# Attention and a gated MLP on one core: the same steps in another order on every engine

## The chip, the cores and the metric

The kernel runs on one core of one Trainium2 chip. The time is device microseconds of one execution, from its start to its end on the core; the median of several executions is compared. The inputs lie in HBM, and so does the output at the end. TensorE (PE) multiplies, VectorE (DVE), ScalarE (ACT) and GpSimd (POOL) work on tiles in SBUF, and SyncE (SP) issues all the transfers (DMAs) of this kernel. Each engine works through its own instructions in order.

## What is computed

For 4 batches, 8 heads and 768 positions of width 64, each chunk of 32 positions attends to 8 memory keys, the 16 positions before it, its own 32 and the 8 behind it. The result, 4 x 768 x 512, goes through a gated MLP with a mixing over positions:

```
scores = 0.125 * q_c @ concat(mem_k, k_ctx).T        # per chunk of 32 queries
a      = softmax(scores);  x = a @ concat(mem_v, v_ctx)
h      = gelu_tanh(x @ w_in)                          # 512 -> 1024
u, v   = h[..., :512], h[..., 512:]
v_n    = (v - mean(v)) / sqrt(var(v) + 1e-6) * g_ln
v_s    = w_sg @ v_n + b_sg                            # over the 768 positions
out    = x + (u * v_s) @ w_out
```

## The kernel before

The large products run in fp32r as three products of parts: each operand is split into a rounded part (hi) and its residue (lo), and hi*lo, lo*hi and hi*hi are accumulated in one PSUM bank (`product`, with `HL`). The residue costs a copy (hi, on ACT) and a subtraction (lo, on DVE or POOL).

All work is cut into 1186 named steps. `step(name, does, *eng)` puts each into a table with its engine, and a few steps with a second engine. The string `ORDER` at the top of the file lists the names; the loop at the end of `conformer_kernel` takes them one after the other and emits their instructions. `InOrder` pins that order, so the order in `ORDER` is the order in which every engine, SP's queue of DMA issues among them, meets its instructions. A star behind a name picks the step's second engine. No planner runs at build time; semaphores are put in from the data that the steps read and write.

The names that matter here:

- `ri<h><k>` loads a 512 KB piece of `w_in` (half h, rows k) as integers. `d3`, `d2`, `d5`, `d6` (ACT, then three DVE passes) turn a piece into fp32, `d8` rounds it (ACT), `d9` makes the residue. For the four pieces `i10` to `i13`, which the V products need, the residue is made on TensorE: `Xi10` and so on subtract by two products, and `d9` only copies from PSUM on ACT. `ro` and `d.o` do the same for `w_out`; `g`, `ga`, `gb` load and split a block of `w_sg`.
- Attention goes by units u = 0 to 23 (6 per batch, 128 positions and 8 heads each). `q<u>`, `k<u>`, `v<u>` load. `S<u>` are the scores: 64 small matmuls, each with its own weight load. `mx`, `sb` (DVE) take the maximum and subtract it, `ex` is Exp on ACT, `z` clears outside keys, `sm`, `sr` (DVE) give the sum and its reciprocal, `nm` multiplies (DVE, or POOL with a star). `T<u>` transposes on TensorE, `p<u>` copies the result to SBUF, `A<u>` multiplies by the values (64 small matmuls with loads). `xc`, `xh`, `xl` copy and split x. `S` of the next unit waits for `sb` of this one, since both touch the same PSUM tile.
- Batch b: `V<b><tt>` is x times the second half of `w_in` for 128 positions, `v1` its Gelu, `v5`, `vx`, `vy`, `v6`, `v7` the normalisation (`v6` on POOL), `v8`, `v9` the split. `U<b><h><j>` is the first half for 384 positions, `u1` its Gelu. `W<b><h><j>` (batches 0 and 1) is the product with `w_sg`, `w1` and `w2` scale and gate it, `w3`, `w4` split it, `O<b><h><j>` is the product with `w_out`, `o1` adds it to x, `out` stores it.
- Batches 2 and 3 take a recombined form of the `w_sg` product: `M<b><term><j>` for seven terms, `mr`, `mt`, `md` (DVE, POOL) add them up, `c1` to `c4`, `sh`, `sl` make the left operands. `y..` steps make the recombined `w_sg` blocks and keep them in HBM.
- `zz<n>` are products of the identity whose result nobody reads.

PSUM has four banks for the products T, X, V, U, W, M and O. `mms` is a queue of free banks: a product takes the first of it, and the step that reads the result last gives the bank back. All steps are emitted in the order of the list, so a product must wait until the step that gave its bank back has run.

```
for i, name in enumerate(names):
    ...
    does, eng = steps.pop(name.rstrip("*"))
    does(eng[name.endswith("*")])
```

Of the kernel before, what the change touches and what calls it, by code (L numbers as in the profile page):

```python
# [51 lines left out]
w2013 w3013 d8o0 d6o2 sm10 d8o2 T8 d9o0* xc7 w4003 w4002 ex11 w2000 w3000 p8 yl010 W012 W010 xc6 yc10 w1012 sb12 d9o2*
sr10 w4000 d9o3 A9 A8 w1010 w2012 w2010 w3010 ex12 yl110 yl100 yc30* z12 O002 O000 o1000 z11 sm11 w4010* nm10 O003
o1003 O001 v12 sm13 sm12 w4013 T10 w3012 w4011 w4012 O013 sr11 xc8 xh6 xc9 xh7 xl7 o1013 yc20 yh50 ym50 k15 v11 out000
S15 k14 S14 O012 mx14 sr13 o1002 mx15 sr12 o1012 O010 xh8 xl8 nm11* o1001 xl6* sb14 T11 o1010 V10 nm13* v110 v510 vx10
sb15 k16 ys50 q17 k17 O011 ex14 p10 q16 V12 ex15 xh9 V11 A10 v112 yh70 yh60 yc40* nm12* yh40 ym60* p11 A11 v111 xl9
ym40 yl001 ys60 T12 p12 o1011 v512 vx12 vy12 v511 xc10 xh10 xc11 V13 vy10 xh11 xl11 v610 v612 v712 v812 xl10 v710 v810
v912* ym70* v910 v113 v513 vx11 yl011 ys40 vx13 vy13 vy11 v613 v713 S16 S17 v813 U102 V15 U101 v115 u1102 v913* v515
V14 out001 U100 v14 yc11* yl111 ys70 q18 yc31* out002 k18 v13 u1101 v114 v611 v711 vx15 vy15 v615 v514 vx14 yh71 vy14
v715 v815 v811 yh51 v614 yc21* v911 T13 v714 v814 u1100 U103 U112 u1103 U111 sm14 mx16 ym51* sr14 p13* nm14* mx17 sb16  # L60
out012 ex16 A12 A13 v915 sm15 v914* W102 sm16 sb17 w1102 sr15 w2102 W100 w1100 w2100 out010 out003 k19 q19 yh61 xc12
w3102 yl101 yc41* ym71 W103 T14 S19 S18 yl002 ys51 k20 cg yl012 w1103 w2103 w4102 mx18 mx19 sb18 v15 W101 ym61* w1101
p14 ex17 w3100 w4100 z17 nm15* w3103 yc12* W112 ex18 u1112 yh41 u1111 w2101 T15 W110 sb19 w1110 ym41* w1112 ys71 yl112
U113 p15 yh52 W113 w3101 w4101 z18 sm18 u1113 xc13 W111 w2112 w1113 w2113 sr18 nm18 w4103* w1111 sm17 sr16 sr17 out013
yl102 yc32* yc22* ym52 A14 A15 O100 U110 q20 ys52 q21 w2111 u1110 w3113 w3111 k21 out011 v17 w2110 w3110 w4110* ys41
ex19 w3112 xc14 yh62 S21 S20 O102 ys61 q22 o1102 O103 nm17* db w4111* w4113 T17 w4112 o1100 p17* mx21 o1103 nm16 O101
o1101 sb21 yh72 O112 xh12 ex21 sm21 xc15 xl12 o1112 sm19 sr19 xh14 O111 T16 O113 yr52 q23 p16* sr21 xl14* v16 v18
out100 yc42* yh42 ym42 k22 yr50 A17 A16 nm19 ym72* o1113 mx20 o1111 T19 sb20 O110 T18 p18* v20 V20 xh13 xl13 V21 S22
xc16 ys72 k23 S23 xh15 ex20 p19 ym62 ys62 ys42 v120 xc17 xl15 mx22 yr51 sb22 sm20 xh17 v121 xh16 out102 v520 ex22 sm22
vx20 vy20 xl16 v620 nm21* V23 sr20 v123 V22 A18 v19 A19 v22 out101 v21 o1110 mx23 sb23 V24 v720 xl17 v521 vx21 out103  # L70
v122 nm20* T21 vy21 U201 ex23 v522 z23 v721 sm23 p21* vx22 vy22 v523 T20 u1201 v124 v622 vx23 v722 v524 vx24 sr23 v724
p20 v723 out113 out110 v621 out112 out111 V25 U200 vz21 xc19 vz20 vz22 vy23 nm23* vy24 sr22 v125 v525 vx25 v725 vy25
sh21 u1200 xc18 v624 v625 vz24 vz25 v623 vz23 nm22* c12* T23 U213 A20 u1213 A21 U203 T22 xc20 sl21* sh22 xc21 U211 p22
A22 c32 p23* v23 A23 yr71 yr60 yr62 yr61 sl22 M220 yr70 sh25 u1203 u1211 yr72 yr41 yr42 yr40 M210 c22* sh26 U202 u1202
sl25 sl26* c42 mr210 mr220 M221 sh24 M251 M211 sh27 mr211 sl27* mr221 M260 w2200* w3200 sl24* mr260 md20 M261 mr261
md21* mr251 sh23 M270 U212 u1212 mr270 M240 mr240 sl23* M271 w4200 M241 w2202 mr271 mr241 w2203 M250 U210 mr250 mt20
w3202 w3203 xc23 w2201 w4202* w3201 w4203* w4201 M230 M231 mt21 mr231 w2212 O201 w3212 mr230 w2211 w2213 o1201 w4212*
u1210 w2210 w3210 w3213 O200 w4213* w4210* w3211 w4211* O203 O202 xh18 xh19 xc22 o1203 O210 o1210 o1202 xl18* O213
O212 o1212 o1200 xl19 O211 xh20 xl20* V32 v132 v532 xh21 xl21* o1213 vx32 v732 V31 xh22 xh23 xl23 V30 v131 v130 v531
vx31 v731 V35 xl22* vy31 vy32 v632 vz32 v135 v535 vx35 vy35 v530 vx30 v730 vy30 V34 v134 v630 v631 v534 vx34 V33 v133  # L80
vz31 vz30 sh31 v635 v533 vx33 vy34 v634 out201 U312 o1211 vy33 v633 v734 v733 vz33 vz34 v735 vz35 c13 c33 u1312 U303
U301 U300 u1301 U302 u1303 sh32 out213 sl31* M310 out210 out212 u1300 sh35 M311 U313 c23 sh36 u1302 u1313 sl32* M321
sl35 M320 c43 sl36* mr310 mr320 sh37 sl37* w2300* w3300 sh34 mr311 mr321 sl34* M350 M361 mr361 md31* w2301* w3301 M371
M360 mr360 md30 mr371 mr350 sh33 M370 mr370 M340 mr340 mt30 M341 mr341 sl33 M351 M331 M330 w4301 w2303 w3303 w4303
mr351 mt31 w2313* w2312* mr330 out211 w2302 w3302 w4302* U310 u1310 w4300* w2310 mr331 U311 O303 O302 O301 u1311 w2311
w3312 w3310 w4310* O300 out200 w3313 w3311 o1303 o1301 w4311* o1300 out203 out300 w4312 w4313 O312 out303 out202
# [660 lines left out]
```

## Time and profile before

| what | value |
|---|---|
| median of 3 runs | 383.28 us (382.34 to 384.22) |
| the profiled execution | 382.99 us, span 381.2 us |
| TensorE busy | 364.7 us, 96% |
| DVE, ACT, POOL busy | 231.3, 168.0, 125.1 us |
| mean granted TensorE clock | 0.991 |
| DMA | 56.01 MB, mean 147 GB/s |
| TensorE's first instruction, its last product's end | 1.35 us, 377.4 us |
| wait of the first scores for their keys | 1.5 us |
| the four transposes of one T step | 0.58 us |
| packets of the queue `q8 instruction` | 37, 0.61 MB |

The span goes from the first to the last instruction of the program; the rest of the execution's time lies around it. Since nearly all steps are emitted from one line of a helper, the profile's line number is the same for all (L99), and groups are told apart by their tiles: `ma` to `mh` are the `w_in` pieces being decoded (`mc` is i12, `md` i13, `ma` i10, `mb` i11, `me` i00), `s` the scores, `av` the values' PSUM tile, `mma` to `mmd` the four PSUM banks. PEld are weight loads, PE the matmuls. The releaser that a wait names is inferred from semaphores, and is the last one to come by the profile, not always the true one. "issue" is waiting that no instruction of another engine explains. [...]

### The profile page before, as it was taken

The page shows a single profiled execution, that of the slowest core. Times are in us where ns is not written, and L with a number is a line of the kernel's source. Part 1 is how long each engine was busy: PE and PEld are TensorE (multiplying, and loading weights), DVE is VectorE, ACT ScalarE, POOL GpSimd, SP SyncE. Part 2 cuts the span into 40 slices and gives each one's busy share as a digit, 9 for nine tenths or more (in the row PEclk, how much of TensorE's full clock was granted, in tenths as well). Part 3 has the DMA queues.
Part 4 walks back from the last instruction along what each step waited for, and adds up shares of the span by engine and source line. Part 5 has one row for each costly group of instructions (what it writes and reads, how often), then busy time and mean ns, then how long its engine had stood idle before and what let it go on. Part 6 is the DMA issues. An engine that isn't in the chain of part 4 may idle for free.

```text
span 381.2 us, 10928 instructions
## 1 busy us (share of the span) xinstructions
PE 364.7 (96%) x4786; PEld 335.9 (88%) x4786; DVE 231.3 (61%) x420; ACT 168.0 (44%) x288; POOL 125.1 (33%) x138
## 2 busy tenths in 40 slices
...
GB/s 283 368 360 163 362 178 93 296 250 131 137 90 160 199 71 132 301 98 23 206 183 217 227 256 85 226 66 124 252 2 21 0 64 0 64 0 1 2 47 139
DMA packets 26063, 56.01 MB, mean 147 GB/s; under 512 B 3232, under 2 KB 13472, under 8 KB 26016
## 3 DMA queue, kind: packets, MB, share of 16 engines
q1 hardware_dynamic: 26016, 55.33, 42.5%
q8 instruction: 37, 0.61, 0.7%
...
## 4 chain that ended last, share of the span: by engine, by line
PE 88%; DVE 5%; ACT 2%; issue 2%; DMA 1%; SPq 0%; POOL 0%; ACTq 0%
PE mmc L99 23%; PE mma L99 19%; PE mmb L99 19%; PE mmd L99 16%; PE av L99 6%; PE s L99 4%; DVE vn L99 2%; DMA ka<-in_ks 1%; ACT L99 1%; ACT vn L99 0%; DVE me L99 0%; DVE eb L99 0%; DVE ea L99 0%; DVE mxa L99 0%; DVE paira L99 0%
## 5 line engine op out<-in xcount | busy, mean ns | idle before, releaser
L99 ACT ACT_TABLE_LOAD x20 | 25.7, 1283 | 9.1 <-DVE xa L99 4.8
L99 ACT CAST vh<-vn 128x768 fp32r<-128x768 f32 (+1 forms) x26 | 18.7, 736 | 18.6 <-DVE vn L99 10.3
L99 PE MATMUL mmc<-w_sg_hi,vh 128*128 128x384 f32 x120 | 25.5, 339 | 1.1 <-ACT uh L99 1.1
L99 DVE BATCH_NORM_STATS2 stats<-vn 128x6 f32<-128x512 f32 x24 | 16.4, 685 | 13.8 <-ACT vn L99 13.8
L99 POOL TENSOR_TENSOR stats<-stats,mhalf 128x1 f32<-128x1 f32 x24 | 15.2, 643 | 25.1 <-DVE stats L99 25.1
L99 PEld LDWEIGHTS mmc<-w_sg_hi,vh 128*128 128x128 f32 x120 | 21.0, 188 | 1.7 <-ACT uh L99 1.5
L99 DVE TENSOR_TENSOR vh<-vn,vh 128x768 fp32r<-128x768 f32 (+1 forms) x18 | 16.6, 927 | 5.7 <-ACT vh L99 5.7
L99 PEld LDWEIGHTS s<-ka,qa 64*32 64x32 f32 x768 | 8.6, 105 | 10.1 <-issue 5.0
L99 POOL TENSOR_TENSOR vh<-vn,vh 128x512 fp32r<-128x512 f32 (+1 forms) x8 | 13.3, 1663 | 10.1 <-ACT vh L99 10.1
L99 DVE TENSOR_SCALAR vn<-vn,stats 128x512 f32<-128x512 f32 x12 | 10.2, 854 | 9.5 <-POOL stats L99 9.5
L99 PE MATMUL s<-ka,qa 64*32 64x64 f32 x768 | 10.6, 225 | 5.3 <-DVE eb L99 2.1
L99 PE MATMUL mmb<-w_sg_hi,vh 128*128 128x384 f32 x66 | 14.1, 340 | 0.0
L99 PE MATMUL mmb<-w_in_hi,paira 128*128 128x512 f32 x48 | 13.2, 397 | 0.0
L99 PE MATMUL mma<-w_sg_hi,vh 128*128 128x384 f32 x60 | 12.9, 338 | 0.0
L99 PE MATMUL mmc<-w_sg_lo,vh 128*128 128x384 f32 x60 | 12.5, 334 | 0.0
L99 POOL TENSOR_TENSOR pairb<-xd,pairb 128x512 fp32r<-128x512 f32 x4 | 5.1, 1284 | 21.2 <-ACT pairb L99 21.2
L99 DVE TENSOR_TENSOR vn<-vn 128x768 f32<-128x768 f32 x6 | 8.9, 1480 | 5.3 <-POOL vn L99 3.8
L99 PEld LDWEIGHTS mmb<-w_sg_hi,vh 128*128 128x128 f32 x66 | 11.5, 188 | 0.2
L99 DVE SCALAR_TENSOR_TENSOR vn<-vn,stats,g_row 128x512 f32<-128x512 f32 x12 | 11.2, 954 | 0.1
L99 POOL TENSOR_TENSOR pairb<-xb,pairb 128x512 fp32r<-128x512 f32 x4 | 5.3, 1335 | 18.1 <-ACT pairb L99 18.1
L99 PE MATMUL mma<-pairb,w_out_hi 128*128 128x384 f32 x56 | 10.9, 335 | 0.0
L99 PEld LDWEIGHTS s<-kb,qb 64*32 64x32 f32 x768 | 8.4, 105 | 2.7 <-DVE ea L99 1.3
...
## 6 DMA issues: line engine op xcount, KB each, us to landing
...
```

What stands on the lines that cost most here:

```text
L99: return self.tc.keep_in_program_order(getattr(self.engine, name)(*args, **kw))
```

## The change

The list `ORDER` is replaced as a whole; nothing else is touched. Both lists hold the same 1186 names with the same three `zz` steps. They differ in the order on every engine, and in which steps carry a star. The start of the diff:

```diff
--- before.py
+++ after.py
 ORDER = """
-ri13 d3i13 d2i13 d5i13 q0 k0 d6i13 d8i13 zz8 S0 mx0 sb0 ex0 z0 sm0 sr0 nm0* k1 q1 ri11 zz4 ri12 S1 zz8 q2 k2 d3i11 mx1
-d2i11 d3i12 d2i12 d5i11 sb1 d5i12 ex1 d6i11 S2 T0 ri10 d3i10 p0 sm1 sr1 d6i12 v0 mx2 sb2 Xi13 A0 d2i10 d5i10 nm1* q3
-k3 d8i12 T1 S3 ex2 d9i13 d8i11 p1 xc0 xh0 mx3 sm2 sb3 d6i10 sr2 Xi12 q4 k4 Xi11 ex3 d9i11 d8i10 d9i12 S4 sm3 sr3 v1 A1
-Xi10 ri00 mx4 sb4 nm2* nm3* q5 k5 ri03 T2 T3 xh1 xl1 xl0 S5 d3i00 d2i00 d5i00 d9i10 p2 d3i03 p3 xc1 ex4 d6i00 mx5
-d2i03 d5i03 V01 v2 ri02 ri01 d6i03 sb5 d3i02 A2 xh2 ex5 d2i02 xl2 d5i02 V00 d8i00 d8i03 d3i01 z5 d9i00* d9i03* d2i01
-d5i01 d6i01 k6 q6 k7 q7 V02 S6 S7 v100 d8i01 d6i02 d8i02 v3 A3 v101 v102 g41 g00 d9i01* d9i02* g21 v5 g10 g01 g20 ga00
-xc3 xh3 ga21 v4 sm4 sr4 U000 U002 ga41 sm5 xl3 sr5 v500 vx00 nm4 mx7 v501 vx01 vy01 sb7 vy00 T4 U003 ro0 k9 q9 g50 g51
-k8 p4 ga20 gb00 nm5* T5 mx6 v600 gb20 ga10 xc2 A4 gb10 p5 u1003 A5 xc4 V03 v700 v502 vx02 vy02 v602 v702 xh4 v800 xc5
-xl4* v601 v701 v802 sb6 V04 g30 q8 cb S8 v801 v902* v901* xh5 v103 xl5* ga50 v104 ga01 ex6 S9 v503 k11 g40 v504 gb21*
-vx03 vy03 v900* gb50 q11 q10 k10 ro1 v603 ex7 vx04 z6 sm6 sr6 vy04 sm7 V05 v105 v505 U001 u1001 u1002 sr7 v604 gb01
-nm7* gb41 ga30 vx05 mx9 sb9 v704 g31 U013 ga40 T7 p7 vy05 mx8 v703 sb8 v803 v605 gb30 v705 v903* gb40* U010 u1010 v805
-ga51 v905 S10 S11 d3o0 v804 v904* u1000 d3o1 d2o0 d2o1 d5o1 d6o1 v6 U011 v7 ex8 g11 q13 v8 U012 d5o0 k12 q12 k13 ga31
-gb51* mx11 mx10 d6o0 W002 u1011 W003 w1002 w2002 nm6* T6 sb10 sb11 ro2 ro3 gb31 ex9 u1012 W001 w1003 w2003 sm9 sr9 p6*
-S13 S12 ga11 d8o1 d9o1* d3o3 sm8 gb11 W011 d2o3 sr8 w1001 d5o3 d6o3 w2001 w1011 nm9* T9 A7 A6 yl000 q15 q14 w3003 mx12
...
+ri12 d3i12 d2i12 zz8 d5i12 d6i12 d8i12 q0 k0 S0 k1 q1 mx0 sb0 ex0 z0 sm0 ri10 d3i10 sr0 d2i10 d5i10 nm0* zz4 S1 mx1
+sb1 ri13 d3i13 d2i13 ri11 d3i11 d2i11 d6i10 d8i10 zz8 k2 q2 ex1 k3 q3 T0 S2 Xi10 S3 d5i11 d6i11 d5i13 d6i13 sm1 p0
+d9i10 d8i13 d8i11 v0 Xi12 Xi13 mx2 sb2 mx3 sr1 sb3 ri03 q4 k4 nm1* ex2 d9i12 ex3 A0 xh0 d3i03 S4 sm2 sr2 T1 v1 p1 Xi11
+sm3 mx4 xl0 d2i03 sr3 d9i11 d5i03 sb4 ri01 nm2* d9i13 T2 p2* A1 V00 k5 v2 d3i01 d2i01 q5 ri02 nm3 d6i03 T3 d5i01 xc1
+xc0 ex4 xh1 xl1 d3i02 d6i01 ri00 S5 mx5 d2i02 d5i02 A2 d8i01 d8i03 V01 xh2 sb5 xl2 g11 k6 q7 k7 d3i00 d2i00 d5i00
+d6i00 d6i02 q6 d9i03* v100 v101 d8i00 d8i02 d9i00* d9i01 d9i02* V02 S7 S6 v102 g50 ga50 ex5 xc2 U001 U003 g20 g31 sm4
+v4 g40 v502 v501 mx7 sr4 vx02 mx6 v500 v3 ga31 p3 ga11 nm4* T4 p4 vy02 sb7 vx01 vy01 ex7 A3 sb6 z5 v602 gb50* sm5 sr5
+A4 k9 q9 k8 ga40 q8 U002 ex6 xc3 ga20 xh3 xc4 xh4 gb40 nm5 v601 v701 xl3 T5 p5 S9 S8 xl4* u1003 z6 mx8 vx00 vy00 v702
+v600 sm6 sr6 sm7 V03 v802 v902 v801 g41 g00 ga00 g30 v5 A5 ga30 v103 mx9 gb31* v700 V04 xc5 v901 ro1 k11 U000 v503 xh5
+v800 u1001 ga41 k10 q11 q10 v104 sb9 gb30* gb20* nm6 sb8 vx03 vy03 xl5 v603 v504 vx04 v703 T6 v900 S11 S10 ex9 V05 p6*
+gb00 g10 ga10 v803 v105 mx10 sr7 vy04 v604 sb10 sm9 v704 mx11 ro0 v6 v7 nm7* gb11 v903 v804 U012 cb q12 g51 T7 p7
+u1012 v505 vx05 vy05 gb10* v904* v605 d3o1 d2o1 d5o1 v705 sr9 ga51 v805 gb51* v905* A6 A7 U013 d3o0 u1013 q13 U010 v8
+sb11 d6o1 d8o1 u1002 ex8 u1000 gb41* g21 ga21 k13 W000 W001 w1000 d2o0 ro3 g01 k12 ga01 W003 gb01* w1001 w2000 d5o0
+w1003 w2003 d6o0 sm8 sr8 nm8 w2001 U011 u1011 nm9* gb21* W002 T9 S12 w3003 d8o0 d9o0* xc6 xc7 w4003 S13 d3o3 ro2 w3001
+ex10 w4001 w1002 d2o3 d5o3 w2002 d9o1 w3002 u1010 d3o2 W010 mx13 d6o3 p9* d2o2 d5o2 d6o2 d8o2 d8o3 w1010 sb13 ex13
+w3000 w4000 W012 W013 W011 yl000 k14 d9o3* w2010 w1011 T8 p8 v9 yl010 yl110 k15 d9o2 A9 w1013 w2011 w3011 A8 v11 q14
+w4002 w1012 w4011* yc10 yh50 w2012 xc8 w3012 yc30* sm10 yc20 sr10 mx12 w4012* O001 O003 o1001 w3010 w4010* w2013 q15
+O000 yh60 ex11 nm10 O002 xh7 o1000 sb12 xl7* yl100 T10 z11 sm11 o1003 p10* yl001 v12 yl011 S14 S15 yl111 q17 cg ym50*
+ys50 V11 xh6 w3013 w4013* v111 xc9 xl6 V10 v110 v510 vx10 mx14 sb14 v511 vx11 yc40 out003 v10 o1002 vy10 xh8 xl8* vy11
...
```

The steps of TensorE alone, read off from the two lists up to the first products with `w_sg`:

```
before: zz8 S0 zz4 S1 zz8 S2 T0 Xi13 A0 T1 S3 Xi12 Xi11 S4 A1 Xi10 T2 T3 S5 V01 A2 V00 V02 S6 S7 A3
        U000 U002 T4 U003 T5 A4 A5 V03 V04 S8 S9 V05 U001 U013 T7 U010 S10 S11 U011 U012 W002 W003
after:  zz8 S0 zz4 S1 zz8 T0 S2 Xi10 S3 Xi12 Xi13 A0 S4 T1 Xi11 T2 A1 V00 T3 S5 A2 V01 V02 S7 S6
        U001 U003 T4 A3 A4 U002 T5 S9 S8 V03 A5 V04 U000 T6 S11 S10 V05 U012 T7 A6 A7 U013 U010 W000
```

The steps of DVE, up to its last subtraction for the first half of `w_in`:

```
before: d2i13 d5i13 d6i13 mx0 sb0 sm0 sr0 mx1 d2i11 d2i12 d5i11 sb1 d5i12 d6i11 sm1 sr1 d6i12 mx2 sb2 d2i10
        d5i10 mx3 sm2 sb3 d6i10 sr2 sm3 sr3 mx4 sb4 xl1 xl0 d2i00 d5i00 d6i00 mx5 d2i03 d5i03 d6i03 sb5 d2i02
        xl2 d5i02 d9i00 d9i03 d2i01 d5i01 d6i01 d6i02 d9i01 d9i02
after:  d2i12 d5i12 d6i12 mx0 sb0 sm0 sr0 d2i10 d5i10 mx1 sb1 d2i13 d2i11 d6i10 d5i11 d6i11 d5i13 d6i13 sm1
        mx2 sb2 mx3 sr1 sb3 sm2 sr2 sm3 mx4 xl0 d2i03 sr3 d5i03 sb4 p2 d2i01 nm3 d6i03 d5i01 xl1 d6i01 mx5
        d2i02 d5i02 sb5 xl2 d2i00 d5i00 d6i00 d6i02 d9i03 d9i00 d9i02
```

The last steps of TensorE:

```
before: M331 M330 U310 U311 O303 O302 O301 O300 O312 O311 O313 O310
after:  U313 M331 M350 M330 O300 O301 O302 O303 O313 O311 O312 O310
```

## Rows read from the trace of the kernel before

**Rows 1.** The page: busy time of TensorE (us, share, instructions), and ACT's table loads.
```profile
PE 364.7 (96%) x4786; PEld 335.9 (88%) x4786; DVE 231.3 (61%) x420; ACT 168.0 (44%) x288; POOL 125.1 (33%) x138
L99 ACT ACT_TABLE_LOAD x20 | 25.7, 1283 | 9.1 <-DVE xa L99 4.8
```

**Rows 2.** Stretches: length, then busy us of each engine, granted clock, DMA share, GB/s.
```profile
12.00:14.00 2.00, 0.13 (x16) 0.13 (x23) 2.00 (x5) 0.15 (x1) 0.00 (x0) 1.00 0.99 392
26.00:28.00 2.00, 0.00 (x0) 0.00 (x0) 1.93 (x5) 0.01 (x1) 0.00 (x0) 0.50 1.04 417
44.80:78.30 33.50, 33.26 (x606) 30.39 (x592) 25.66 (x53) 23.91 (x44) 16.73 (x19) 1.00 0.63 206
83.00:377.40 294.40, 294.40 (x3398) 279.88 (x3398) 171.11 (x309) 117.93 (x201) 101.39 (x97) 1.00 0.34 115
```

**Rows 3.** TensorE's waits over the span: us in total, times, longest us.
```profile
PE mmb L99 <- DVE me L99: 4.4, 1, 4.4
PE s L99 <- DVE eb L99: 2.1, 1, 2.1
PE s L99 <- issue: 1.5, 1, 1.5
PE mmc L99 <- ACT uh L99: 1.1, 1, 1.1
```

**Rows 4.** Timeline around the two stops: start, us, engine, operation, idle time before.
```profile
20.69 0.68 DVE L99 SCALAR_TENSOR_TENSOR ma<-rawa,ma 128x512 uint32<-128x512 uint32 x1
21.81 0.62 ACT L99 CAST w_in_hi<-ma 128x512 fp32r<-128x512 f32 x1
22.89 0.84 PE L99 MATMUL s<-ka,qa 64*32 64x64 f32 x63 [1.50 <-issue]
24.72 0.19 PEld L99 LDWEIGHTS mmb<-ma,ident 128*128 128x128 f32 x1
29.18 1.86 PE L99 MATMUL mmb<-ma,ident 128*128 128x512 f32 x2 [4.39 <-DVE me L99]
```

**Rows 5.** The stretch between the two stops, columns as in group 2.
```profile
22.85:29.15 6.30, 1.91 (x127) 1.90 (x128) 4.39 (x7) 1.21 (x3) 0.82 (x1) 0.75 1.01 400
```

**Rows 6.** DMA queues from 22.9 to 26.8, then 26.8 to 27.9: packets, MB, share.
```profile
q1 hardware_dynamic: 444, 1.55, 99.9%
...
q8 instruction: 1, 0.02, 5.3%
```

**Rows 7.** The chain that ended last: start us, us, what (steps of each kind).
```profile
18.05 0.79 PE s L99 x53
18.84 1.29 PE mmd L99 x3
29.18 2.29 PE mmb L99 x3
33.85 2.93 PE mmd L99 x12
36.78 1.06 PE av L99 x64
46.01 2.28 PE mma L99 x12
297.57 2.08 PE mma L99 x12
314.09 2.72 PE mmc L99 x12
```

**Rows 8.** Timeline of the start, DVE and the third score step.
```profile
11.27 1.01 DVE L99 TENSOR_SCALAR mb<-mb 128x512 int32<-128x512 int32 x1
12.20 0.41 DVE L99 TENSOR_SCALAR mc<-mc 128x512 int32<-128x512 int32 x1
13.87 0.86 PE L99 MATMUL s<-ka,qa 64*32 64x64 f32 x64 [2.14 <-DVE eb L99]
```

**Rows 9.** Timeline, the first W product.
```profile
78.50 1.20 PE L99 MATMUL mma<-w_sg_hi,vh 128*128 128x384 f32 x6
```

More of the change, by code (lines that the diff above doesn't have):

```diff
@@ L47 @@
-nm7* gb41 ga30 vx05 mx9 sb9 v704 g31 U013 ga40 T7 p7 vy05 mx8 v703 sb8 v803 v605 gb30 v705 v903* gb40* U010 u1010 v805
-ga51 v905 S10 S11 d3o0 v804 v904* u1000 d3o1 d2o0 d2o1 d5o1 d6o1 v6 U011 v7 ex8 g11 q13 v8 U012 d5o0 k12 q12 k13 ga31
-gb51* mx11 mx10 d6o0 W002 u1011 W003 w1002 w2002 nm6* T6 sb10 sb11 ro2 ro3 gb31 ex9 u1012 W001 w1003 w2003 sm9 sr9 p6*
-S13 S12 ga11 d8o1 d9o1* d3o3 sm8 gb11 W011 d2o3 sr8 w1001 d5o3 d6o3 w2001 w1011 nm9* T9 A7 A6 yl000 q15 q14 w3003 mx12
-d8o3 nm8 d3o2 W013 w2011 w3011 w3001 w4001* v9 v10 u1013 d2o2 mx13 sb13 ex13 ex10 p9* w3002 d5o2 w1013 W000 w1000
@@ L52 @@
[L52 to L86, printed above, removed]
@@ L87 @@
-out301 O311 o1312 o1311 o1302 out311 out312 O313 o1313 O310 out302 out313 o1310 out310
+ri12 d3i12 d2i12 zz8 d5i12 d6i12 d8i12 q0 k0 S0 k1 q1 mx0 sb0 ex0 z0 sm0 ri10 d3i10 sr0 d2i10 d5i10 nm0* zz4 S1 mx1
+sb1 ri13 d3i13 d2i13 ri11 d3i11 d2i11 d6i10 d8i10 zz8 k2 q2 ex1 k3 q3 T0 S2 Xi10 S3 d5i11 d6i11 d5i13 d6i13 sm1 p0
+d9i10 d8i13 d8i11 v0 Xi12 Xi13 mx2 sb2 mx3 sr1 sb3 ri03 q4 k4 nm1* ex2 d9i12 ex3 A0 xh0 d3i03 S4 sm2 sr2 T1 v1 p1 Xi11
+sm3 mx4 xl0 d2i03 sr3 d9i11 d5i03 sb4 ri01 nm2* d9i13 T2 p2* A1 V00 k5 v2 d3i01 d2i01 q5 ri02 nm3 d6i03 T3 d5i01 xc1
@@ new lines @@
+v611 v711 sr11 ex12 O013 O011 z12 o1013 mx15 yc11 nm11* yc31* O010 V12 v112 v512 vx12 O012 yh40 q16 o1012 yc21 ym40*
+ym60 xh9 yh70 U100 T11 A10 u1100 p11 v811 A11 o1010 xl9* vy12 sb15 ex15 xc10 xh10 ym70 v610 v710 sm13 sr13 v612 nm13*
+U102 v810 xc11 ex14 xh11 V13 sm12 o1011 xl10* v911* sm14 xl11* V14 k17 k16 out000 yl101 ys40 v113 yh61 T13 v712 u1102
+v812 v912* v513 v910 S17 S16 v114 V15 v115 v514 U101 v515 vx15 vx14 vy15 sr12 nm12* v615 vx13 vy14 v614 vy13 v613 v715
+v714 v13 out001 U103 u1103 v815 q19 ys70 p13 v814 u1101 U112 U113 yc41 ym61* ys61 k18 T12 sm15 v915* v713 mx17 v813
@@ new lines @@
+ys60 k19 p12 yh51 A13 A12 v14 q18 v15 out013 mx16 v913* sr15 v914 ym51* W100 w1100 nm15* yh71 u1112 out002 W101 W112
+w1101 w2100 w3100 sb17 sb16 ym71* w1112 w2112 w2101 u1113 w3101 T15 S18 S19 mx18 mx19 sr14 nm14 sb19 W103 w1103 w4101*
+W102 U110 w2103 w3103 T14 w4103* p15* w1102 w2102 sb18 xc13 xc12 U111 w3102 u1111 p14* ex16 sm16 w4100* ex17 ex19
+w3112 W113 W110 z17 yl002 yl012 yc12 sm17 ys51 yh41 ex18 sr16 w1113 out012 ys71 yh52 v16 nm16* yl112 k20 W111 sm19
+w1110 sr19 w2113 w1111 w2111 T16 ym41 w3111 w4111* A15 A14 q20 out011 yl102 k21 q21 sr17 z18 w4102 sm18 sr18 u1110
@@ new lines @@
+nm17* O102 p16* w2110 out010 w3110 xc15 w4112* w4110* O101 db T17 yc32* yc22* S20 o1101 S21 O103 O100 w3113 xc14 w4113
+yr50 ys41 k23 k22 mx21 sb21 o1102 O112 mx20 sb20 p17* o1112 yc42 xh14 yh62 ym52 O113 O111 o1113 o1103 nm19 ex20 out102
+v17 ys52 yr51 yh42 ym42* nm18 T19 A17 A16 xh12 xl12 p19* o1100 v18 ym62* sm20 sr20 yr52 q23 q22 ex21 sm21 o1111 out100
+O110 V20 xc17 ys42 T18 yh72 xh13 xl13* ym72 xc16 xh16 xl16 xh15 p18 S23 S22 V21 sr21 nm21 nm20* xl15 mx23 sb23 ex23
+z23 xh17 xl17 xl14 sm23 out103 ys62 out111 ys72 v120 v121 mx22 sb22 ex22 sm22 V23 v521 vx21 vy21 sr22 sr23 v520 vx20
@@ new lines @@
+v20 vy20 out112 v123 v19 out113 out101 T20 A18 A19 V22 v122 v523 v522 vx22 vy22 V25 v125 v722 v720 vx23 v525 o1110
+vx25 v721 v620 v621 vz20 v723 vy23 nm22 v622 vz22 p20 xc19 U202 V24 v124 u1202 xc18 v21 v22 T21 U200 p21* v524 vx24
+T22 A20 A21 xc20 vz21 sh21 U201 U213 vy25 p22* v625 v623 out110 xc21 v725 nm23 T23 A22 p23 v23 A23 yr60 sl21* vz23
+v724 vy24 v624 vz24 vz25 c12 u1200 U212 u1212 u1213 c32 c22 u1201 M210 sh22 U203 u1203 sh26 U211 u1211 sh25 sl25 yr62
+yr71 sl22* c42 sl26* M211 mr211 mr210 M221 sh27 sl27 M220 mr220 yr61 M260 mr260 md20* w2200 mr221 sh24 sl24 w2201*
```

12 lines of the change are left out of this document (added).

## Prediction

> **What bounds the kernel now.** I began with the busy shares of the page. TensorE is busy for 364.7 of the 381.2 us of the span [rows 1], and no other engine passes 61%. Its busy share in stretches then shows where the rest lies: from 83.0 to 377.4 us it is busy for all 294.40 us, with the clock at 1.00 [rows 2]. An order of the same products can hardly gain there; it can only lose. What can be won lies before 83 us. The list of TensorE's waits has it [rows 3]: 4.4 us before the product Xi10, 2.1 and 1.5 us before score steps, 1.1 us at 82.9 us. With the first wait for keys, 1.5 us in the table of the profile, the first 1.4 us and some 3.8 us behind the last product, which the new list keeps (the same first transfer, the same warm-up steps, the same last product, add and store), that is nearly all of the 16.5 us.
>
> The longest wait is put down to DVE's work on `me`, but Xi10 doesn't read `me`. It reads `ma` and its rounded copy, and these were done at 21.4 and 22.4 us [rows 4]. The matmul began at 29.18. The second look is at counts: S4 stopped after one of its 64 matmuls and went on with 63 at 22.89, Xi10 stopped after its first weight load, and between the two stops lie 127 matmuls and 128 loads [rows 4, 5]. Stops that are 255 instructions apart, whatever the instructions are, with all data there, are instruction fetches. In the same stretch the transfer queues moved data alone until 26.8 us; then one packet of the instruction queue passed, and TensorE went on about 1.4 us after it [rows 6]. So one block was started at 22.89 and the next was there at 29.18: 6.3 us for a block that S4 and A1 use up in under 2 us.
>
> [...]
>
> [...]
>
> **The change.** The new list has the same 211 TensorE steps, and the same matmuls (4786 with the warm-up). Only order and engine assignment differ: by count of the two lists DVE gets 439 steps in place of 420, POOL 107 in place of 123, ACT 263 in place of 266; and switches between Exp and Gelu go from 20 to 22, each a table load of 1.28 us [rows 1], 2.6 us more for an engine that is busy 44%. These cost nothing while TensorE is fed; the slower rival prices the other case.
>
> *Where the block borders fall.* A score or value step is 128 instructions, a transposing step 8, X 6, U, V and O 24, W 36, M 18. The two stops come after 696 and 952 instructions; borders further on follow every 256. In the new list 440 falls in S3, 696 is 10 instructions into S4 and 952 lies near the end of A1. Between 696 and 952 there are now S4, T1, Xi11, T2 and A1: 0.8 + 0.6 + 1.3 + 0.6 + 0.95 = 4.2 us [rows 7] (the 0.58 of a T step stands in the table of the profile) instead of 1.9. So this stop shrinks by at least 2.3 us, to 2.1 us if the fetch again takes 6.3, to nothing if it takes 4.2. At that time the new list has issued about 9.8 MB of loads (all eight w_in pieces, six q/k pairs, three v, one w_sg block), which at the traced rate are through at about 29 us, much like before. I take 1.5 us.
>
> *The start, followed by hand.* Until S2 at 13.9 us [rows 8] little differs: S0 waits for the same keys, and S2 for sb1, which again stands behind two w_in passes on DVE, the first slowed from 0.41 to 1.01 us [rows 8]; only T0 now fills 0.6 us of TensorE's idle time. Then DVE has two shifts at 0.41 and eight passes at 0.69 (five for three w_in pieces, then sm1, mx2, sb2) [rows 4, 8], and ends them at 20.2. S3 waits for sb2, so TensorE idles from 17.4 (end of Xi10) to 20.2. That is worse than before, where S3 ran at 18.05 [rows 7]. Then: S3 to 21.1, Xi12 and Xi13 to 23.7, A0 to 24.8, S4, T1, Xi11, T2 to 28.1, A1 with the stop of 1.5 us to 30.6, and V00 there, where before the first V came at 33.85 [rows 7]. V00, T3, S5, A2 end at 35.8, V01, V02, S7, S6 at 42.8. DVE in that time: sb3 at 22.8, mx4 behind S4 and xl0 to 27.0, four small steps and sb4 to 29.0, five passes to 32.1, then xl1, d6i01, mx5, d2i02, d5i02, sb5, xl2 to 37.9, 2.5 us of w_in passes and three subtractions, 42.5. So U001 can start at 42.8. Before, U000 started at 46.0 [rows 7] with one value step more done (A3, 1.06 us). **Gain: 46.0 - 42.8 - 1.1 = 2.1 us**, between 0.9 (both fetches at 6.3 us and a further 0.6 us of waiting) and 3.6 (no stop).
>
> *From U001 to W000.* Seven U, three V, five A, four S, four T: 14.6 + 8.2 + 5.3 + 3.2 + 2.3 = 33.6 us, and 0.3 for changes between shapes: W000 at 76.7. Before, the first W stood at 78.5 [rows 9], with U011 more and T6, A6, A7 less behind it, 0.6 us; the lead is kept or grows a little. The wait of 1.1 us at 82.9 us was for the bank of U012, whose Gelu stood behind a score's Exp and a table load. In the new list u1012 comes behind v804 and p7, with no Exp between. I count it gone: -1.1 us, bounds -1.1 and 0.
>
> *Behind 83 us.* Before waits nowhere there. I counted, for each product, how much TensorE work lies between the last product that used its PSUM bank and itself: under 2.2 us in 19 places before, in 25 in the new list (among them W002 behind the gate of W003, and O300 behind mr350). Reading a bank out takes one or two DVE passes, up to 1.4 us at 0.69 [rows 4], so all are covered by a hair; one more pass in the queue leaves a few tenths open. From 0 to 3 us in all; I take 0.7, nearer to the 0 that the 19 cost.
>
> *Sum.* The profiled execution took 383.0 us (span 381.2, 1.8 around it), the median is 383.3, so the two can be used alike. 383.0 - 2.1 - 1.1 + 0.7 = **380.5 us**.
>
> **The rivals.**
> A: little is left. The idle stretch from 17.4 to 20.2 is as long as gaps get in this trace without data or instructions, and the clock fell right behind such a phase before [rows 2]. At half clock Xi12 and Xi13 take 1 us more each [rows 7]; the next border stops at its full 2.1. That eats the 2.1 us of the start, and two of the narrow banks the 1.1: 382.7. For it: a gap of 2.9 us. Against: the gap of 2.1 us before S2 left it at 1.00 [rows 2, 3].
> B: slower. DVE becomes the bound from 42.5 us until W000. Its 59 steps there (49 before, to the same two points) are 25 full-width passes at 0.69, 16 of 0.42 to 0.66 and 18 short ones: 29.9 us. W000 at 76.7 needs DVE at 87% of the time; from 44.8 to 78.3 it reached 25.66 of 33.5 us, 77% [rows 2]. At 77% it needs 38.8 us, W000 comes at 81.3, 4.6 us late, and the wait at 82.9 stays in another place: 383.0 - 2.1 + 4.6 = 385.5. It decides at 82%, where the lead is just used up. Against it: at 77% TensorE was still busy for 33.26 of those 33.50 us, so DVE's gaps were no lack of time.
> C: much faster. Fetches are ready in time, DVE keeps up, nothing is lost behind: 3.6 at the start, 1.1, and the 0.6 by which the lead may grow up to W000: 377.7.
> That the order has nothing to win from fetches at all (383.0) has no chance of its own beside the stops of [rows 4].
>
> **How the numbers follow.** The forecast's own case 0.42 (378.5 to 382), A 0.27, B 0.17, C 0.14. A change is told from none here at about 0.5%, 1.9 us, so faster is below 381.4 and slower above 385.2. Faster: C and nearly nine tenths of the forecast's case, 0.52. Slower: most of B and a little of A, 0.17. Within: 0.31. The range goes to B's 385.5 and to 376.6, a us below C, since a count by hand over 40 us can be off by that.
>
> **What would show it.** Right: no TensorE idle time over 2.2 us before 31 us except before S3; a stop near the end of A1 of 1 to 2 us; the first V at about 30.6 and the first U at about 42.8; W000 near 76.7; no wait behind that over 0.5 us. Wrong: the first V behind 33 us, or a stop in S4 as well (the 440 border's fetch late); the clock at 0.50 between 19 and 30; DVE as the releaser of W000 or of S8 to S11; and, against all that, a wait of several us behind 83 us, which no row of before announces.

## The result, and the profile after

The new list takes 380.07 us (median of 6 runs, 379.17 to 381.01) where the list before, on the same chip, takes 383.75 (382.34 to 386.03): a ratio of 0.990, interval 0.9865 to 0.9935. The forecast was 380.5. The profiled execution took 380.16 us, span 378.4.

The page of the new list (busy time and share) and its table loads, which answer to [rows 1]:

```profile
PE 367.0 (97%) x4786; PEld 337.9 (89%) x4786; DVE 236.3 (62%) x439; ACT 169.6 (45%) x287; POOL 110.3 (29%) x122
L99 ACT ACT_TABLE_LOAD x22 | 28.2, 1283 | 5.3 <-PE mmd L99 2.2
```

TensorE is busy 2.3 us longer with the same 4786 matmuls, and its idle time falls from 16.5 to 11.4 us: 5.1 less idle, 2.3 more busy, 2.8 us of span. Where TensorE still idles is in its waits (total, times, longest), against [rows 3]:

```profile
PE s L99 <- DVE ma L99: 2.5, 1, 2.5
PE av L99 <- issue: 1.8, 1, 1.8
PE mma L99 <- POOL mhalf L99: 1.4, 1, 1.4
PE s L99 <- DMA ka<-in_ks: 1.1, 1, 1.1
PE mmd L99 <- issue: 0.9, 1, 0.9
PE mmc L99 <- DVE ed L99: 0.2, 1, 0.2
```

The stops of 4.4 and 1.5 us and the wait of 1.1 us at 82.9 are gone. The wait before S2 has stayed (2.1 before, 2.5 now). One stop of 1.8 has come in A1, and one of 0.9 at 205.9 us that was not there. The timeline of the new list's TensorE shows them, and the points that the forecast named (start, us, operation, number, idle time before):

```profile
15.18 0.85 PE L99 MATMUL s<-ka,qa 64*32 64x64 f32 x64 [2.47 <-DVE ma L99]
...
17.84 1.19 PE L99 MATMUL s<-kb,qb 64*32 64x64 f32 x64
22.88 0.86 PE L99 MATMUL s<-ka,qa 64*32 64x64 f32 x64
25.78 1.06 PE L99 MATMUL av<-pt,vb 64*64 64x32 f32 x57
28.65 0.32 PE L99 MATMUL av<-pt,vb 64*64 64x32 f32 x7 [1.81 <-issue]
28.89 1.20 PE L99 MATMUL mma<-w_in_hi,paira 128*128 128x512 f32 x4
29.93 1.66 PE L99 MATMUL mma<-w_in_lo,paira 128*128 128x512 f32 x4
31.38 1.91 PE L99 MATMUL mma<-w_in_hi,paira 128*128 128x512 f32 x4
...
76.80 1.20 PE L99 MATMUL mmd<-w_sg_hi,vh 128*128 128x384 f32 x6
...
204.21 0.79 PE L99 MATMUL mmd<-paira,w_out_lo 128*128 128x384 f32 x3
205.94 0.44 PE L99 MATMUL mmd<-paira,w_out_lo 128*128 128x384 f32 x1 [0.94 <-issue]
...
216.36 0.66 PE L99 MATMUL mmc<-ident,ed 128*128 128x128 f32 x4 [0.24 <-DVE ed L99]
```

S2 stands at 15.18, S3 at 17.84, S4 at 22.88, A1 stops after 57 of its 64 products, V00 begins at 28.89, W000 at 76.80. V00's three groups of four products take 1.20, 1.66 and 1.91 us: the granted clock, 1.00 at full speed, fell inside it. The stretches of the new list say so (columns as in [rows 2]), and also that DVE was busy for 85% of the time from the first U to the first W while TensorE lost nothing:

```profile
16.50:20.00 3.50, 3.50 (x70) 1.74 (x68) 2.76 (x5) 1.91 (x4) 0.00 (x0) 0.51 0.91 334
28.90:33.30 4.40, 4.40 (x18) 3.40 (x15) 1.85 (x3) 3.50 (x7) 0.15 (x1) 0.65 0.11 40
42.80:76.80 34.00, 33.99 (x723) 30.80 (x713) 28.98 (x60) 25.05 (x43) 18.56 (x20) 1.00 0.79 256
83.00:374.50 291.50, 290.31 (x3261) 277.05 (x3260) 174.15 (x322) 115.22 (x196) 86.11 (x82) 1.00 0.34 114
```

The queues answer to [rows 6]. From 23.0 to 26.1 us data alone moved; the block's packet passed in the next 1.1 us (it begins at 26.19):

```profile
q1 hardware_dynamic: 431, 1.26, 103.1%
...
q1 hardware_dynamic: 121, 0.43, 98.1%
q8 instruction: 1, 0.02, 5.2%
```

### The profile page after: what moved, and what is told of

The parts are those of the page before. It is cut to its first block, busy times and chain, and to the rows that moved or that the text cites. A ratio compares the mean times of both kernels' runs of the same rounds, so it can differ in the third digit from the quotient of the medians.

```text
span 378.4 us, 10930 instructions
## 1 busy us (share of the span) xinstructions
PE 367.0 (97%) x4786; PEld 337.9 (89%) x4786; DVE 236.3 (62%) x439; ACT 169.6 (45%) x287; POOL 110.3 (29%) x122
## 4 chain that ended last, share of the span: by engine, by line
PE 94%; DVE 2%; DMA 1%; issue 1%; SPq 0%; ACT 0%; POOL 0%
PE mma L99 22%; PE mmb L99 21%; PE mmd L99 21%; PE mmc L99 18%; PE av L99 6%; PE s L99 5%; DMA ka<-in_ks 1%; DVE ma L99 1%; DVE ed L99 0%; SPq L99 0%; DVE rda L99 0%; DVE mxa L99 0%; DVE ea L99 0%; ACT ea L99 0%; DVE xd L99 0%
## 5 line engine op out<-in xcount | busy, mean ns | idle before, releaser
L99 POOL TENSOR_TENSOR vh<-vn,vh 128x512 fp32r<-128x512 f32 (+1 forms) x12 | 19.9, 1667 | 15.4 <-ACT vh L99 15.4
L99 PE MATMUL mmc<-w_sg_hi,vh 128*128 128x384 f32 x102 | 21.2, 334 | 0.0
L99 DVE TENSOR_TENSOR vh<-vn,vh 128x768 fp32r<-128x768 f32 (+1 forms) x14 | 13.5, 961 | 4.7 <-ACT vh L99 4.5
L99 PE MATMUL mmd<-w_sg_hi,vh 128*128 128x384 f32 x66 | 13.9, 338 | 0.0
L99 PE MATMUL mmb<-w_in_hi,pairb 128*128 128x512 f32 x48 | 12.9, 390 | 0.0
L99 ACT ACTIVATE vn<-mmb 128x512 f32<-128x512 f32 x9 | 5.4, 598 | 16.4 <-PE mmb L99 15.6
L99 DVE TENSOR_TENSOR vn<-vn 128x768 f32<-128x768 f32 x6 | 5.8, 958 | 9.9 <-POOL vn L99 6.3
L99 PEld LDWEIGHTS mma<-w_sg_hi,vh 128*128 128x128 f32 x66 | 11.6, 188 | 0.1
L99 PEld LDWEIGHTS mmd<-w_sg_hi,vh 128*128 128x128 f32 x66 | 11.5, 188 | 0.1
L99 PE MATMUL av<-pt,vb 64*64 64x32 f32 x512 | 9.2, 220 | 1.8 <-issue 1.8
```

Source lines behind the costliest of these rows:

```text
L99: return self.tc.keep_in_program_order(getattr(self.engine, name)(*args, **kw))
```

## The experiments

Each kernel ran 6 to 12 times beside the list before on one chip, in four groups. The new list itself ran again in three of them, as a yardstick: 0.9883 (0.9837 to 0.9929), 0.9916 (0.9893 to 0.9938) and 0.9881 (0.9856 to 0.9907). All three had the stop in A1 behind 57 products, of 2.0, 2.3 and 1.6 us.

> The changed kernel itself, as the yardstick beside the kernel before on one chip. Expected: 380.1 us, 0.990 of before, again with a stop of about 1.8 us inside A1 (57 of 64 products done), a stop of about 0.9 us behind S20 and S21, the first V near 28.9 and the first U near 42.8 us. If the stops are instruction fetches, they fall on the same instruction again; if they are something of one execution, they move or go.

> The new list itself, as the yardstick of the three kernels beside it: about 380 us, ratio to the old list 0.988 to 0.991. Both theories of the start have the stop in A1 again, after 57 of its 64 products, of 1.8 to 2.0 us.

> The new list itself once more, as the yardstick of the two kernels beside it: ratio to the old list 0.988 to 0.992, the stop in A1 after 57 products again, 5.7 to 6.2 us behind the start of S4 (27.9 to 28.7 us).

**Two steps of the list before, one at a time and together.** First A1 alone:

```diff
-S4 sm3 sr3 v1 A1 Xi10 ri00 mx4 sb4 nm2* nm3* q5 k5 ri03 T2 T3 xh1
+S4 sm3 sr3 v1 Xi10 ri00 mx4 sb4 nm2* nm3* q5 k5 ri03 T2 T3 A1 xh1
```

> The kernel before with a single step moved: A1 behind Xi10, T2 and T3 instead of ahead of Xi10, on TensorE alone. The block of 256 instructions that S4 and A1 used up then also holds Xi10, T2 and T3, 2.5 us of work. Theory (fetch borders): the stop of 4.4 us moves into A1 and shrinks by the 2.5 us that now lie ahead of it, to about 2 us; the first V starts at about 30.8 instead of 33.8, the first U near 43.5 and the whole takes 380.5 to 381 us, 2.5 to 3 less than before, nearly as much as the whole new list gives. Rival (the gain comes from the new order of DVE's and SP's work, and the stop only covers a wait for data that would show in its place): the first V stays at 33 or later, and the time within 0.3% of before.

Measured 382.44 us, ratio 0.9978 (0.9947 to 1.0008): not to be told from the list before, and not the 380.5 to 381 us that I had said. By the time alone the rival would stand; its other sign, a first V at 33 us or later, did not come. TensorE's timeline of this kernel:

```profile
24.35 1.01 PE L99 MATMUL av<-pt,vb 64*64 64x32 f32 x54
28.16 0.64 PE L99 MATMUL av<-pt,vb 64*64 64x32 f32 x10 [2.80 <-issue]
30.19 2.07 PE L99 MATMUL mmd<-w_in_hi,paira 128*128 128x512 f32 x4 [0.28 <-DVE paira L99]
32.06 1.91 PE L99 MATMUL mmd<-w_in_lo,paira 128*128 128x512 f32 x4
```

The stop left Xi10, which had all its data in both lists, and went into A1, where the count puts the border: so the 4.4 us of [rows 3] was an instruction fetch, and not DVE's `me`. It kept 2.8 us where I had said 2, and V01, the first V here, ran slowly behind it: 2.07 and 1.91 us for four products, as V00's last four in the new list, 1.91 at a measured clock of 0.50. In this profile the first U came at 44.61, 1.3 us ahead of the list before (43.5 said).

Then DVE's step gb51 alone:

```diff
+gb51*
 d2o0
...
-gb51*
```

> The kernel before with a single step moved on DVE: gb51, which frees the buffer that the Gelu of U011 takes, ahead of the w_out decoding (d2o0 to d5o0) instead of behind it. Theory (the wait of 1.1 us at 82.9 us is a chain DVE, buffer, ACT's Gelu, PSUM bank, W003): the wait goes, 1.1 us less than before, about 382.2 us, 0.997. Rival (W003 would wait for something else at once, for DVE or ACT are the bound there): a wait of like size stays within 5 us of 82.9, and the time is that of before.

Measured 381.21 us, ratio 0.9945 (0.9919 to 0.9971). The timeline of the list before shows the chain that made the wait; `uh` is the buffer of gb51's block and then of U011's Gelu:

```profile
80.44 0.55 DVE L99 TENSOR_TENSOR w_sg_lo<-uh,w_sg_hi 128x384 fp32r<-128x384 f32 x1
81.08 1.28 ACT L99 ACT_TABLE_LOAD   x1 [2.44 <-DVE w_sg_lo L99]
82.38 0.49 ACT L99 ACTIVATE uh<-mmc 128x384 f32<-128x384 f32 x1
82.92 1.31 PE L99 MATMUL mmc<-w_sg_hi,vh 128*128 128x384 f32 x6 [1.14 <-ACT uh L99]
```

With gb51 moved, these are the same residue and the same Gelu, and no wait follows:

```profile
75.86 1.40 DVE L99 TENSOR_TENSOR w_sg_lo<-uh,w_sg_hi 128x384 fp32r<-128x384 f32 x1
...
79.84 0.49 ACT L99 ACTIVATE uh<-mmc 128x384 f32<-128x384 f32 x1
...
81.52 1.20 PE L99 MATMUL mmc<-w_sg_hi,vh 128*128 128x384 f32 x6
```

ACT's idle 2.44 us was a wait for a buffer. The gain is 2.1 us where I had said 1.1; its interval reaches from 1.1 to 3.1. The profiles account for 1.6 of it: besides the wait, W003 took 3.13 us in place of 3.40 and W001 3.13 in place of 3.33. Why these two are shorter is not shown.

Both moves in one list:

> The old list with two steps moved: A1 behind Xi10, T2 and T3, and gb51 on DVE ahead of d2o0. Theory (the two places where the old list lost its time explain the result): the gains of the two moves add up, 0.85 + 2.1 us as measured alone, about 380.6 us, ratio 0.990 to 0.994, so within 1 us of the new list; the wait before the first Gelu of U011 is gone and the 4.4 us stop is 2 to 3 us. Rival (the new order of all the rest carries the gain): ratio stays at 0.996 or more, at least 2 us behind the new list.

Measured 380.01 us, ratio 0.9925 (0.9896 to 0.9954), beside 0.9916 of the new list on that chip. The product of the two ratios alone is 0.9923. Within what these runs can tell, two moved steps do what the new order of 1186 does; of the two, gb51 alone is clear of the noise. The way there differed: S4 stopped for 2.5 us and A1 for 0.7, where A1 late alone had none and 2.8:

```profile
23.86 1.05 PE L99 MATMUL s<-ka,qa 64*32 64x64 f32 x63 [2.53 <-issue]
...
30.05 0.41 PE L99 MATMUL av<-pt,vb 64*64 64x32 f32 x10 [0.68 <-issue]
```

The first U stands at 44.06 with A3 done; the new list's at 42.84, and 1.06 us of A3 to come, is 43.90.

**What the fetch waits for.** In the next kernel a load is moved forward on SP, k6, whose buffer comes free late, so that three loads behind it, 1.2 MB together, are held back (issued at 24.68 to 27.08 us; at 20.85 to 21.95 in the new list).

```diff
-q5 ri02 nm3 d6i03
+q5 k6 ri02 nm3 d6i03
...
-xl2 g11 k6 q7
+xl2 g11 q7
```

> The changed kernel with one issue moved on SP: k6, which waits for S4, ahead of ri02, ri00 and g11, so that these 1.2 MB are issued behind S4 (about 24 us) instead of at 21 to 22 us. The order of TensorE stays. Theory (a fetch waits for the transfers that were queued before it): the block asked for when S4 begins (about 23 us) finds 3 us less ahead of it, its packet passes by about 25 us instead of 26.2, and the stop in A1 falls from 1.8 to 0.5 us or less; the first V starts at about 27.5, and the time is 1 to 2 us under the changed kernel (378 to 379). Rival (a fetch takes its 5 to 6 us whatever is queued): the stop stays at 1.8 us. Second rival: the later loads make the decoding on ACT and DVE late, and the first U comes later than 43.5 us.

Measured 378.11 us, ratio 0.9875 (0.9827 to 0.9922), beside 0.9883 of the new list: no difference that can be told. A1 ran whole, as the theory had it, and the first U came at 40.97, so the second rival's delay did not come. But V00 came at 28.54, not 27.5, for a stop appeared one border earlier, in S4:

```profile
21.55 0.30 PE L99 MATMUL s<-ka,qa 64*32 64x64 f32 x5 [0.32 <-DVE ed L99]
23.14 1.13 PE L99 MATMUL s<-ka,qa 64*32 64x64 f32 x59 [1.29 <-issue]
27.48 1.14 PE L99 MATMUL av<-pt,vb 64*64 64x32 f32 x64
```

After TensorE went on at 23.14, 239 data packets in 1.7 us passed until the instruction packet for A1's block came at 24.8, where the first profile of the new list had 431 in 3.1. That agrees with the theory that fewer transfers waiting make a shorter fetch; that the earlier fetch was late in this run is not explained by the move.

Then Xi11 (1.3 us) is taken out of the block that ends in A1, by a move ahead of S4, and in another kernel ahead of A0:

```diff
-sb3 ri03 q4 k4 nm1* ex2 d9i12 ex3 A0 xh0 d3i03 S4 sm2 sr2 T1 v1 p1 Xi11
+sb3 ri03 q4 k4 nm1* ex2 d9i12 ex3 A0 xh0 d3i03 Xi11 S4 sm2 sr2 T1 v1 p1
```

> The new list with Xi11 moved ahead of S4. The 256 instructions that end in A1 then hold S4, T1, T2 and A1, 1.3 us of work less, and they begin 1.1 to 1.3 us later. Theory (the next block is asked for when TensorE enters a block, and takes 5.7 to 6.3 us at this load): the stop in A1 grows by what was taken out of the block, from 1.8 to 2.0 us to 2.9 to 3.3 us, still after 57 of 64 products, and V00 comes 1.1 to 1.3 us later than beside it. Rival 1 (the block comes at a fixed time, when the transfers of that time are through): the stop ends when it did, 27.9 to 28.7 us, and V00 comes no later. Rival 2 (the stop has a fixed length or is a wait for data): 1.8 to 2.0 us again.

> The new list with Xi11 moved further ahead than before, in front of A0: between it and the border in S4 now stand the 128 small instructions of A0. The move to right ahead of S4 had left 4.4 us from the start of S4 to the end of the stop, where the list unchanged has 5.7 to 6.2. Theory (the next block is asked for when TensorE's sequencer, not its matmul, crosses the border, and the sequencer runs a few instructions ahead; Xi11's six slow ones covered 1.3 us, A0's small ones cover 0.1): 5.7 to 6.2 us behind the start of S4 again, so the stop grows to 2.8 to 3.4 us, and V00 comes 0.7 to 1.3 us later than in the list unchanged. Rival (the block comes when the transfers of that time are through, whenever it is asked for): the stop ends at 27.9 to 28.7 us as in every run of the new list so far, 2 us long or less, and V00 comes no later.

Measured 379.58 us, ratio 0.9917 (0.989 to 0.9943) beside 0.9916, and 379.98, ratio 0.9915 (0.989 to 0.994) beside 0.9881. TensorE of the first of them:

```profile
24.18 0.86 PE L99 MATMUL s<-ka,qa 64*32 64x64 f32 x64
26.46 1.03 PE L99 MATMUL av<-pt,vb 64*64 64x32 f32 x57 [0.41 <-ACT pt L99]
28.61 0.32 PE L99 MATMUL av<-pt,vb 64*64 64x32 f32 x7 [1.12 <-issue]
```

The stop shrank to 1.12 where I had said 2.9 to 3.3, and V00 came at 28.86, 0.24 us behind the list beside it: the fixed delay from entering a block falls here, and the rival's time held. In the second kernel S4 came no later (22.10). Its stop was 2.28 us, neither the 2.8 to 3.4 of the theory nor the rival's 2 or less, and ended at 27.69; V00 came at 28.06, no later than beside it (28.30), which is the rival's sign. From the start (or second start) of S4 to the end of the stop, with the start of the instruction packet that passed in between:

| kernel | S4 | packet | stop ends | S4 to end |
|---|---|---|---|---|
| A1 late alone | 21.16 | 25.71 | 28.16 | 7.0 |
| new list, 4 profiles | 21.84 to 22.88 | 25.69 to 26.19 | 27.93 to 28.65 | 5.5 to 6.2 |
| Xi11 ahead of A0 | 22.10 | 25.31 | 27.69 | 5.6 |
| list before (stop in Xi10) | 22.89 | 26.87 | 29.18 | 6.3 |
| k6 moved forward | 23.14 | 24.82 | no stop | |
| gb51 alone (stop in Xi10) | 23.61 | 27.21 | 29.64 | 6.0 |
| A1 late and gb51 | 23.86 | 27.63 | 30.05 | 6.2 |
| Xi11 ahead of S4 | 24.18 | 26.41 | 28.61 | 4.4 |

A fixed time of arrival doesn't hold either (27.7 to 30.1). What the packets do show is that these stops were waits for instructions: in each of the 15 stops before 31 us, in 12 profiles, TensorE went on 2.2 to 2.5 us after the packet began, whichever step stood there and whichever releaser was named. What varies is the time from S4 to the packet, 1.7 to 4.6 us; it was shortest where loads were held back, but with none held back it was once 2.2 us too (Xi11 ahead of S4). When a block is asked for, no trace shows, so the 6.3 us of the prediction and the 444 data packets of [rows 6], counted over 16 engines, are not shown to be a queue that the fetch stood in: with Xi11 ahead of S4, the packet of S4's own block began at 18.27, before S3 (18.52), in which the border before it lies. What orders a block's packet among the data stays open.

**A version that fills the block.** V00 has its operands before A1 does its work, and takes 2.7 us with 24 instructions; O103 can part S20 from S21.

```diff
-p2* A1 V00 k5
+p2* V00 A1 k5
...
-S20 o1101 S21 O103 O100
+S20 O103 o1101 S21 O100
```

> The new list with V00 moved ahead of A1, and O103 moved between S20 and S21. Theory: V00 has its operands when T2 ends (the last residue is written at about 25.6 us and is read in its second third), so the block that ends in A1 holds 2.7 us more work, about 6.7 us in all, and the stop of 1.8 to 2.0 us goes to under 0.3; T3, S5 and A2 come 1.8 to 2.4 us earlier. The stop behind S21 (0.9 and 0.4 us in the two profiles) goes too, since the block that held the 128 + 128 small instructions now holds 2.1 us of O103 as well. Together 2.2 to 2.9 us, about 377.5 us, ratio to the old list 0.981 to 0.985. Rival (the lead is given back before the first U, since DVE's passes on the pieces of w_in end no earlier): U001 starts at 42.5 us or later, and the time is 379 to 380 us, at most the 0.4 to 0.9 us of the later stop gained.

Measured 378.78 us, ratio 0.9879 (0.9848 to 0.991) beside 0.9916 (0.9893 to 0.9938). The intervals overlap, and the 0.981 to 0.985 that I had said was missed. Its waits of TensorE:

```profile
PE av L99 <- DVE paira L99: 1.5, 1, 1.5
...
PE s L99 <- DVE rdc L99: 1.2, 1, 1.2
```

No wait for an instruction is left, in A1 or behind S21 (there three of seven profiles without the move of O103 had none either). U001 came at 42.07. A part of the gain went into a wait of A2 for xl1, and S4 began 1.2 us late, by the trace for DVE's `rdc`, which it doesn't read; its keys, issued at 16.6, landed after 6.6 us, at 23.2, and it began at 23.4. Two further kernels move xh1, which xl1 needs, forward on ACT. The first put it right behind A1, ahead of `d3i01`:

> The new list with V00 ahead of A1, O103 between S20 and S21, and xh1 on ACT right behind A1, ahead of xc1, xc0 and Exp of unit 4. With the first two alone the stops were gone, but A2 waited 1.5 us for xl1, which stood behind xh1, and xh1 behind three other passes of ACT. Theory: xl1 ends 1.3 to 1.5 us earlier, A2 follows S5 with under 0.3 us of idle time, U001 starts at 40.6 to 41.2 us, and the kernel takes 377 to 378 us, ratio 0.983 to 0.986. Rival (DVE and POOL, which end the pieces of the first half of w_in, set U001 or U003): U001 or the U behind it waits for a residue, U001 not before 41.8, and the ratio stays at 0.988.

Measured 381.24 us, ratio 0.9933 (0.9902 to 0.9965), beside 0.9881 (0.9856 to 0.9907) of the new list on that chip: worse, at the edge of what the runs can tell, where 0.983 to 0.986 had been said. The profile is of a run of 384.06 us, near the slowest of the 12 (378.49 to 384.92). The decoding of `mf` stood behind xh1 on ACT, and so behind A1, and nm3 behind `mf` on DVE:

```profile
21.58 0.30 PE L99 MATMUL s<-ka,qa 64*32 64x64 f32 x5
24.52 1.01 PE L99 MATMUL s<-ka,qa 64*32 64x64 f32 x59 [2.63 <-issue]
...
35.09 1.11 PE L99 MATMUL mmb<-ident,ed 128*128 128x128 f32 x4 [2.33 <-DVE ed L99]
```

The 2.33 us are this mistake's. The 2.63 us before it are not: up to there the order is the new list's. The second kernel has xh1 behind that decoding:

```diff
-d5i01 xc1 xc0 ex4 xh1 xl1
+d5i01 xh1 xc1 xc0 ex4 xl1
```

> The new list with V00 ahead of A1, O103 between S20 and S21, and xh1 ahead of xc1, xc0 and Exp of unit 4 on ACT, but this time behind the decoding of the piece mf, which the earlier place had held up (nm3 stood behind it on DVE, and T3 lost 2.3 us). Theory: no wait before T3, A2 follows S5 with under 0.4 us of idle time in place of 1.5, U001 at 40.6 to 41.2 us where no fetch stops S4, and 377 to 378.3 us, ratio 0.983 to 0.987. Rival 1 (DVE and POOL set the first U's): a wait of a U for w_in_lo takes the 1.2 us back, 378.8 us. Rival 2: S4 stops for its block, as in one profile of three of this family, though the list up to there is unchanged; then U001 is 1 to 2.6 us later and the runs spread over 4 us or more.

Measured 377.12 us (375.95 to 378.81), ratio 0.9839 (0.9814 to 0.9864), the fastest of the lists here, and faster in each of its 6 runs than the median of the new list in any group (379.45 to 380.07). The new list did not run beside it; by the ratios to the list before, the interval is clear of one yardstick (0.9893 to 0.9938) and overlaps the other two. TensorE of this kernel:

```profile
22.47 0.86 PE L99 MATMUL s<-ka,qa 64*32 64x64 f32 x64
28.12 1.14 PE L99 MATMUL av<-pt,vb 64*64 64x32 f32 x64
31.67 1.13 PE L99 MATMUL av<-pt,vc 64*64 64x32 f32 x64 [1.03 <-DVE paira L99]
40.48 0.97 PE L99 MATMUL mma<-paira,w_in_lo 128*128 128x384 f32 x4
```

U001 at 40.48 is where the theory had it, but A2 still waits 1.03 us, not under 0.4: xl1 began at 30.92, when xc1 and xc0 had ended on ACT (30.89); why it waited for them is not shown. From the start of A1 to A2 this kernel takes 3.55 us, the one before it 4.05 (29.20 to 33.25), so xh1 is worth 0.5 us. The other 1.1 us by which U001 is earlier lie ahead of A1, where the two lists are the same: there the other kernel's S4 had waited for its keys.

## Why the prediction was right

The two places that were to gain did gain: the start and the wait at 82.9 us, and moving one step at each gives the same time. That the sum of 380.5 comes within 0.4 us of the profiled execution (380.16) is in part luck. The terms as measured, -2.1, -1.1 and +1.2, make 381.0. Of the other 0.8 us, 0.4 lies behind the last product, where I had said that nothing changes (3.8 us to the end of the span before, 3.4 now); W003, 0.3 us shorter without the stop before it, is a part of the rest. Term by term:

- *The start, 2.1 us said.* U001 came at 42.84 (42.8 said); with A3's 1.06 against [rows 7] that is 2.1. But two errors met in it. I had S3 wait for sb2 until 20.2: that was misread from the list, where S3 stands ahead of mx2 and sb2, and it ran at 17.84. That S waits for sb of the unit before holds only where sb stands ahead of it in the list. So V00 came at 28.89, not 30.6, though the stop was longer than said. Then V00 took 4.33 us (28.96 to 33.29 by the chain) at a mean clock of 0.65 (0.50 in its last part, from 31.38 us), 1.3 us more than in the yardstick with V00 at full clock (2.99). I had charged half clock to rival A alone. The size was right, the way to it was not. S2 too came 1.3 us later than said (15.18 for 13.9). The wait before it is put down to DVE's `ma`; in two of the yardsticks the same wait, of 2.4 and 2.3 us, is put down to the load `qa`. On SP four pieces of `w_in` now stand ahead of that load where there were three, which I had not followed.
- *The stop, 1.5 us said, in A1 near its end.* 1.81 there, 1.6 to 2.3 in the yardsticks. The count held: for the 256 instructions of a block that I went by, the trace of before has 255 between its two stops [rows 5], and in the new list 254 lie between the place where S4 stopped in two kernels of its order (6 loads, 5 products done) and the stop in A1 (58 loads, 57 products). The 6.3 us from S4 to the end of the stop that I took as fixed are 4.4 to 7.0. Fetches did not hold TensorE up everywhere: from 83 to 204 us it was busy for all 121.00 us, while in S4, Xi10, A1 and behind S21 it waited 0.3 to 4.4 us in one profile or another.
- *From U001 to W000, 33.9 us said.* 33.96. DVE was busy for 28.98 us, close to the 29.9 that I had counted, at 85%: rival B's 77% was a habit of the old list, no bound.
- *The wait at 82.9 us, 1.1 us said.* Gone, 1.1 of its term by the trace. The reason was half wrong: it was U011's bank, and the Gelu stood behind a buffer that gb51 read, not behind Exp alone.
- *Behind 83 us, 0.7 said for narrow PSUM banks.* No product waited for a bank. 1.2 us were lost to other things: 0.24 is the transposing step T19, which waited for DVE's `nm19` at 216.36, and 0.94 is an instruction stop behind S20 and S21, which together are 256 instructions by the list and last about 1.5 us (202.75 to 204.28). Its packet began at 203.49, 2.45 us before TensorE went on; in four of the seven profiles with this order here the stop fell behind the same three products; the other three had none, and neither had the three with O103 between the two steps. By count of the list this place is not a multiple of 256 behind the stop in A1; whether instructions that the trace does not list lie between is not shown. I looked for borders up to A1 only, and named a stop behind 83 us as something that "no row of before announces".

Not all of the signs fit. Three that I had named for being right failed: TensorE idled 2.5 us before S2 (2.2 allowed), the first V came at 28.9 (30.6), and a stop behind 83 us took 0.94 (0.5). One for being wrong, rival A's, did appear: the clock at 0.51 between 16.5 and 20.0. The loss that it was to bring was paid by S3's earlier start. (Rival A's 2.8 us were not "as long as gaps get" either: [rows 3] has one of 4.4.) The runs do not show that the rest of the new order adds anything: the list before reaches its time with two steps moved.
